# Side taps of a 3x3 convolution: rows read as unbroken runs of 64, column planes swapped by the accumulator's address pattern

## Chip, cores, metric

One core of a Trainium2 chip. The metric is the device time of one execution in microseconds (us); lower is better. A matmul's "spacing" below is the time from its start to the start of the next matmul, taken from the trace's records of starts. PE is TensorE (PEld its weight loads), DVE is VectorE, ACT is ScalarE, POOL is GpSimd.

## The reference, cut to what matters

```python
def reference(x, t_emb, g1, be1, w1, w_emb, g2, be2, w2):   # x: (2, 512, 64, 64) bf16
    ...                                                     # gn: group norm over 4 groups
    def conv3(z, w):                                        # 3x3, padded, 512 -> 512 channels
        zp = jnp.pad(z, ((0, 0), (0, 0), (1, 1), (1, 1)))
        taps = [jnp.einsum("bchw,oc->bohw", zp[:, :, i:i+H, j:j+W], w[:, :, i, j]) ...]
        ...
    h = conv3(_silu(gn(x, g1, be1)), w1)
    h = h + (_silu(t_emb) @ w_emb).reshape(B, C, 1, 1)
    h = conv3(_silu(gn(h, g2, be2)), w2)
    return x + h
```

## The kernel before

The work is cut into 8 chunks (2 convolutions x 2 images x 2 halves) and 4 units of 128 output channels each. Fast-convolution transforms save matmuls: along rows always, along columns from chunk 1 on. In the trace, chunk 0 ends near 90 us, chunks 1 to 3 near 290 us, chunks 4 to 7 at 486 us. DVE makes the transforms, ACT evacuates PSUM and applies silu.

An image row lies in SBUF as 65 fp16 columns: 32 even pixels, one zero, 32 odd pixels. A "plain" group makes 512 outputs (8 rows, even half then odd half) by three matmuls per input block, one for each column tap `kx`. A side tap makes the even outputs from odd pixels and the other way round, so its read takes the second half of each row first:

```python
RW = 65                                     # row pitch, in elements of 2 bytes
def plain_mms(bank, c, k, ct, s):
    ...
    for i, kx in enumerate((0, 2, 1)):      # the two side taps, then the centre
        ...                                 # w: 128x128 weights
        off, st = ((32, -32), (0, 33), (33, -32))[kx]
        rhs = A(vo + off, [[RW, 8], [st, 2], [1, 32]])
        lst.append((Ps(bank, 0, [[1, 512]]), w, rhs, ct == 0 and i == 0, ct == CT - 1 and i == 2))
```

Every operation is recorded with an assumed cost, and a list scheduler fixes the order on each engine before anything is emitted.

## Time and profile before

| | before |
|---|---|
| time, median of 3 runs | 500.62 us (500.51 to 501.32) |
| profiled span | 500.2 us |
| plain matmuls, 512 columns | 1248, of which 832 side taps |
| spacing of first side tap, second side tap, centre (150 to 475 us) | 228, 227.5, 222 ns |
| spacing of 256 columns; of 512 columns in a row (embedding) | 109 ns; 215 ns |

First the page's line of busy time and the row of the granted clock (40 slices of 12.5 us, tenths of full speed), then the groups of PE by form (busy us, mean ns of one, then idle time just before them and who ended it):

```profile
PE 465.6 (93%) x2853; PEld 276.9 (55%) x2853; DVE 434.1 (87%) x856; ACT 382.5 (76%) x614; POOL 37.8 (8%) x66
...
PEclk9999999988599999999999999999999999999996
```

```profile
line engine op names shapes xcount | busy us, mean ns | idle before us <-releasers
L380 PE MATMUL psum<-ar 128*128 128x512 f16 x1248 | 295.5, 390 | 8.7 <-DVE ar L329 4.3 <-DVE fs L442 2.2 <-ACT ar L352 2.1
L380 PE MATMUL psum<-ar 128*128 128x256 f16 x1408 | 164.8, 274 | 0.2 <-ACT ar L352 0.2
```

Busy time by stretch: window, its length, then busy us and instructions of PE, PEld, DVE, ACT and POOL, then granted clock (1.00 is full), busy share of the DMA engines, GB/s:

```profile
136.00:190.00 54.00, 53.75 (x301) 28.93 (x299) 48.38 (x104) 49.92 (x81) 1.08 (x1) 1.00 0.35 113
190.00:245.00 55.00, 55.00 (x309) 29.64 (x309) 50.63 (x107) 45.34 (x86) 4.75 (x9) 1.00 0.60 188
245.00:305.00 60.00, 60.00 (x360) 34.72 (x359) 59.57 (x114) 48.85 (x76) 1.01 (x7) 1.00 0.78 262
...
395.00:450.00 55.00, 55.00 (x399) 38.57 (x397) 52.82 (x84) 40.01 (x48) 6.24 (x8) 1.00 0.69 166
```

PE is full, yet from 245 to 305 us DVE, with 59.57 of 60, is just as full.

```profile
301.64 2.42 DVE L329 TENSOR_TENSOR ar<-ar 128x2048 f16<-128x2048 f16 x3
303.98 0.16 DVE L442 COPY fs<-psum 128x8 f32<-128x8 f32 x1
304.09 0.69 DVE L329 TENSOR_TENSOR ar<-ar 128x1024 f16<-128x1024 f16 x1
```

The copy stands in DVE's stream without a gap, and PE's first matmul into bank 7 starts at 304.19 us, 0.05 us after the copy ends (from the records of starts and ends). PE is just in time for DVE.

### The profile page before, as it was taken

The page shows a single profiled execution, that of the slowest core. Times are in us where ns is not written, and L with a number is a line of the kernel's source. Part 1 is how long each engine was busy: PE and PEld are TensorE (multiplying, and loading weights), DVE is VectorE, ACT ScalarE, POOL GpSimd, SP SyncE. Part 2 cuts the span into 40 slices and gives each one's busy share as a digit, 9 for nine tenths or more (in the row PEclk, how much of TensorE's full clock was granted, in tenths as well). Part 3 has the DMA queues.
Part 4 walks back from the last instruction along what each step waited for, and adds up shares of the span by engine and source line. Part 5 has one row for each costly group of instructions (what it writes and reads, how often), then busy time and mean ns, then how long its engine had stood idle before and what let it go on. Part 6 is the DMA issues. An engine that isn't in the chain of part 4 may idle for free. (4 is left out here: it accounts for less than half of the span.)

```text
span 500.2 us, 8097 instructions
## 1 busy us (share of the span) xinstructions
PE 465.6 (93%) x2853; PEld 276.9 (55%) x2853; DVE 434.1 (87%) x856; ACT 382.5 (76%) x614; POOL 37.8 (8%) x66
## 2 busy tenths in 40 slices
PE   6999999686699999999999999999999999999980
PEld 5744344253345455555554567666666666666660
DVE  1699999997769999997999999997999999985553
ACT  4886899999699978679987887777765888565440
POOL 3100000000100000110000001103011110011000
PEclk9999999988599999999999999999999999999996
DMA  8754463465723336576576887677676768557232
GB/s 330 281 171 113 156 177 111 167 201 164 237 85 120 119 108 180 171 213 237 201 244 219 294 285 206 167 192 135 194 194 187 201 171 247 108 106 150 44 43 43
DMA packets 41064, 87.17 MB, mean 174 GB/s; under 512 B 6464, under 2 KB 16448, under 8 KB 41024
## 3 DMA queue, kind: packets, MB, share of 16 engines
q1 hardware_dynamic: 35808, 77.07, 46.5%
q0 software_dynamic: 4928, 9.59, 12.9%
q8 instruction: 22, 0.36, 0.3%
q14 instruction: 18, 0.15, 0.1%
q10 hardware_dynamic: 288, 0.01, 0.0%
HBM read 62.25 MB, written 31.85 MB: 188 GB/s over the span
## 5 line engine op out<-in xcount | busy, mean ns | idle before, releaser
L380 PE MATMUL psum<-ar 128*128 128x256 f16 (+2 forms) x2737 | 450.4, 326 | 9.0 <-DVE ar L329 4.3
L329 DVE TENSOR_TENSOR ar<-ar 128x1040 f16<-128x1040 f16 (+6 forms) x682 | 404.9, 651 | 39.5 <-ACT ar L352 35.1
L380 PEld LDWEIGHTS <-ar 128*128 128x128 f16 (+1 forms) x2729 | 264.3, 98 | 192.2 <-issue 16.1
L352 ACT ACTIVATE ar<-ar 128x384 bf16<-128x384 bf16 (+6 forms) x206 | 169.6, 854 | 45.6 <-DVE ar L329 41.6
L352 ACT ACTIVATE ar<-psum 128x512 f16<-128x512 f32 (+2 forms) x221 | 153.8, 718 | 51.1 <-PE psum L380 42.3
L352 ACT ACTIVATE ar<-ar,fs 128x2112 f16<-128x2112 bf16 (+1 forms) x32 | 68.6, 2148 | 6.9 <-DMA ar<-h_scr 5.1
L365 POOL DMA_DIRECT2D out_dram<-ar x16 | 19.3, 1207 | 129.1 <-DVE ar L329 129.0
L333 DVE TENSOR_SCALAR ar<-ar 128x512 f16<-128x512 f16 (+2 forms) x72 | 26.0, 382 | 2.0 <-ACT ar L352 2.0
L352 ACT ACTIVATION_READ_ACCUMULATOR ar<-psum 128x1 f32 x96 | 19.6, 204 | 0.0
L451 POOL TENSOR_TENSOR fs<-fs 128x1 f32<-128x1 f32 (+1 forms) x7 | 7.0, 996 | 138.2 <-DVE fs L449 138.2
L380 PE MATMUL psum<-ar,ones_bf 128*128 128x260 bf16 x64 | 9.5, 307 | 4.7 <-DMA ar<-in_x_dram 4.7
L369 POOL MEMSET ar<- 128x65 f16 (+4 forms) x27 | 4.1, 195 | 114.5 <-DVE ar L329 41.9
L380 PE MATMUL psum<-fs,ones_neg 128*128 128x1 f32 (+3 forms) x36 | 5.2, 258 | 7.0 <-DVE fs L982 6.9
L352 ACT ACTIVATION_READ_ACCUMULATOR ar<-ar 128x1 f32 x56 | 11.0, 197 | 0.0
L380 PEld LDWEIGHTS <-ones_bf 128*128 128x128 bf16 x64 | 6.6, 108 | 6.4 <-issue 3.4
L380 PEld LDWEIGHTS psum<-fs,ones_neg 128*128 128x128 f32 x36 | 5.0, 206 | 8.0 <-DVE fs L982 7.2
L365 POOL DMA_DIRECT2D ar<-ar x4 | 3.7, 930 | 72.3 <-DVE ar L329 56.4
L913 DVE SCALAR_TENSOR_TENSOR ar<-psum,ident 128x128 bf16<-128x128 f32 x4 | 1.2, 290 | 5.6 <-PE psum L380 5.6
L993 DVE BATCH_NORM_STATS2 fs<-ar 128x6 f32<-128x512 bf16 x8 | 5.3, 681 | 0.0
L442 DVE COPY fs<-psum 128x2 f32<-128x2 f32 (+1 forms) x7 | 1.1, 161 | 4.5 <-PE psum L380 4.5
L415 DVE CAST fs<-gparm 128x16 f32<-128x16 bf16 x1 | 0.2, 190 | 2.8 <-DMA gparm<-in_params_dram 2.8
L411 ACT ACT_TABLE_LOAD x1 | 1.3, 1283 | 1.7 <-PEq L1135 1.7
(49 smaller groups left out, 23.4 us busy)
## 6 DMA issues: line engine op xcount, KB each, us to landing
ar<-in_w_dram SPq DMA_DIRECT2D x32, 384.0 KB, 3.9
ar<-in_x_dram SPq DMA_DIRECT2D x16, 552.5 KB, 4.0
h_scr<-ar SPq DMA_DIRECT2D x16, 520.0 KB, 3.2
ar<-h_scr SPq DMA_DIRECT2D x16, 520.0 KB, 4.0
out_dram<-in_x_dram SPq DMA_DIRECT2D x32, 260.0 KB, 4.2
out_dram<-ar POOLq DMA_DIRECT2D x16, 520.0 KB, 6.4
u_scr<-ar SPq DMA_DIRECT2D x16, 384.0 KB, 3.2
ar<-u_scr SPq DMA_DIRECT2D x4, 1536.0 KB, 7.6
```

What stands on the lines that cost most here:

```text
L329: pl.op("DVE", 0.075 + 0.000521 * out.n, lambda: nc.vector.tensor_tensor(out=out.ap, in0=a.ap, in1=b.ap, op=op), regs(a, b), regs(out), name)
L333: pl.op("DVE", cost or 0.075 + 0.00026 * out.n, lambda: nc.vector.tensor_scalar(out=out.ap, in0=a.ap, scalar1=s, scalar2=None, op0=ALU.mul ...
L352: lambda: nc.scalar.activation(out=out.ap, in_=a.ap, func=func, scale=sc, **kw), regs(*rr), regs(*ww), name)
L365: lambda: eng.dma_start(out=out, in_=in_, **kw), regs(*r), regs(*w), name, lat=3.2 if sw else None, after=after, sw=sw)
L369: pl.op("POOL" if eng == "gpsimd" else "DVE", 0.08 + 0.0005 * out.n, lambda: e.memset(out.ap, v), (), regs(out), name)
L380: nc.tensor.matmul(out.ap, lhsT=lhsT.ap, rhs=rhs.ap, start=st, stop=sp, skip_group_check=True)
L411: nc.scalar.activation(out=fs[:, WARM:WARM + 1], in_=fs[:, WARM + 1:WARM + 2], func=ACT.Silu)
L415: nc.vector.tensor_copy(out=fs[:, GB:GB + 4 * CT], in_=gparm[:])
L442: pl.op("DVE", 0.16, lambda: V.tensor_copy(out=F(tot, 2 * n).ap, in_=ps.ap), regs(ps), regs(F(tot, 2 * n)), name)
L451: pl.op("POOL", 0.85, lambda: nc.gpsimd.tensor_tensor(out=F(rs, n).ap, in0=N.ap, in1=F(NEGH, n).ap, op=ALU.pow), regs(N), regs(F(rs, n)), ...
L913: pl.op("DVE", 0.3, lambda: nc.vector.scalar_tensor_tensor(out=j2.ap, in0=g.ap, scalar=1.0 / HW, in1=ident[:], op0=ALU.mult, op1=ALU.mult, ...
L993: pl.op("DVE", 0.61, lambda e=e, q=q: nc.vector.bn_stats(out=q.ap, in_=e.ap), regs(e), regs(q), nm)
```

## The change

The side taps read each row as one run of 64 columns. The swap of the halves moves to the write: the accumulator's pattern puts the first 32 columns of a row 32 places up. Values are the same.

```diff
-            off, st = ((32, -32), (0, 33), (33, -32))[kx]
-            rhs = A(vo + off, [[RW, 8], [st, 2], [1, 32]])
-            lst.append((Ps(bank, 0, [[1, 512]]), w, rhs, ct == 0 and i == 0, ct == CT - 1 and i == 2))
+            if kx == 1:
+                rhs, o = A(vo, [[RW, 8], [33, 2], [1, 32]]), Ps(bank, 0, [[1, 512]])
+            else:
+                rhs, o = A(vo + kx // 2, [[RW, 8], [1, 64]]), Ps(bank, 32, [[64, 8], [-32, 2], [1, 32]])
+            lst.append((o, w, rhs, ct == 0 and i == 0, ct == CT - 1 and i == 2))
```

The scheduler's costs depend on sizes alone, so the order on every engine is unchanged, as the two traces confirm (I compared the recorded operations with their dependences and planned starts: all 2736 are equal).

## The prediction

> **What bounds it now.** The profile page: span 500.2 us, PE busy 93%, DVE 87%, ACT 76%. The table of busy time by stretch shows PE at 10.00 of 10 us in nearly every stretch from 130 to 480 us, but DVE at 9.8 to 10.0 in most of them too. Three phases:
> - 20 to 130 us (plain chunk 0): DVE or ACT is full (DVE 9.4 to 10.0 of 10 from 30 to 100 us, ACT 9.3 to 10.0 from 110 to 130); PE is released by DVE or ACT after gaps of 2.1, 3.3, 6.9 and 2.2 us at 96, 102, 127 and 130 us. DVE/ACT bound.
> - 136 to 486 us: PE issues back to back; what its starts lose against the typical spacing adds up to under 1 us. PE bound, with DVE almost level.
> - 486 to 500 us: a tail without matmuls.
>
> **What the change does.** Same instructions in the same order on all engines (the schedule's costs depend on sizes alone). Of 1248 plain matmuls (128x512), the 832 side taps read 8 runs of 64 instead of 16 runs of 32 with a backward step, and write PSUM in blocks of 32 with swapped order instead of 512 in a row. Weights, bytes and results are unchanged.
>
> **Costs, from the starts of consecutive matmuls in the trace** (150 to 475 us):
> - side tap 228 ns and 227.5 ns; centre tap (16 forward runs) 222 ns; an embedding matmul with 512 unbroken columns 215 ns; 256-column matmuls 109 ns. The Trainium skill, "TensorE: Matmul & The Clock Gate", section Back-to-back issue gap, gives N/2.4 + 2.5 ns, so 215.8 and 109.2: the trace agrees. So a forward break costs about 0.45 ns and a backward one about 0.8.
> - Seven forward breaks: 215.5 + 3 = 218.5 ns, if it counts breaks; 221.5 if only skipped columns count. I take 219.5: 8 ns saved per side tap, 832 x 8 = 6.7 us in all.
> - The write side: the skill's "PSUM — Partial Sum Buffer", section Specifications, says any non-contiguous pattern slows matmuls significantly. This trace disagrees: the 256-column matmuls that write blocks of 32 at pitch 64 and those that write 256 in a row are both at 109 ns. I expect the swapped blocks to be free; the backward order is untried here.
>
> **How much is critical.** PE's starts against the ends of what releases them: PE is pinned to DVE (slack about 0.05 us) at 127, 130, 174, 304 and 390 us, after stretches in which DVE has no gap (145 to 174, 245 to 304, 360 to 394). Side taps there only make PE wait longer. Before 130 us nearly nothing counts. Left: about 380 side taps, 380 x 8 = 3.0 us; 0.2 more from early ACT evacuations.
>
> **Predicted: 497.4 us, range 495.2 to 499.9.** Faster by over 2%: 0.02; within 2%: 0.96; slower by over 2%: 0.02.
>
> **What would show it.** Side-tap spacing 218 to 222 ns, centre tap still 222, 256-column 109. PE busy down by about 6 us; PE's waits on DVE near 127, 174, 304 and 390 us each longer by 0.3 to 1.2 us; DVE's busy time unchanged (434 us), its share up. PE's last matmul about 3 us earlier, tail unchanged at 14 us.
>
> **What would make it wrong.** A backward PSUM step that costs as the backward read did (spacing stays 228: no change, or more: slower); spacing near 215 (gain about 5 us); DVE pins that are looser than I read, so more of the 6.7 us comes through; the half clock granted at 122 to 136 us after PE's wait moving or lasting one period (3.4 us) more or less.

## More of the kernel before

The helpers that matter later:

```python
def tt(out, a, b, op, name=""):             # every add of the transforms, on DVE
    pl.op("DVE", 0.075 + 0.000521 * out.n, lambda: nc.vector.tensor_tensor(...), ...)

def gn_chain(layer, b, ct, mes, name, SB=7, slack=2.5, n=1):   # statistics of a group norm
    ...                                     # small matmuls into PSUM bank 7
    pl.op("DVE", 0.16, lambda: V.tensor_copy(out=F(tot, 2 * n).ap, in_=ps.ap), ...)
    ...                                     # a unit's group 5 uses bank 7 too
```

The gaps of DVE from 190 to 245 us look like room. This one, from the timeline of DVE and then of ACT (start, us, what), decided more than I saw when I predicted:

```profile
225.65 3.04 DVE L329 TENSOR_TENSOR ar<-ar 128x512 f16<-128x512 f16 x6
230.65 1.92 DVE L329 TENSOR_TENSOR ar<-ar 128x1040 f16<-128x1040 f16 x3 [1.96 <-ACT ar L352]
```

```profile
225.70 2.37 ACT L352 ACTIVATE ar<-ar 128x384 bf16<-128x384 bf16 x2
227.94 0.22 ACT L352 ACTIVATION_READ_ACCUMULATOR ar<-ar 128x1 f32 x1
228.03 0.62 ACT L352 ACTIVATE ar<-psum 128x512 f16<-128x512 f32 x1
228.51 0.23 ACT L352 ACTIVATION_READ_ACCUMULATOR ar<-psum 128x1 f32 x1
228.60 2.02 ACT L352 ACTIVATE ar<-ar 128x2145 f16<-128x2145 f16 x1
230.48 0.63 ACT L352 ACTIVATE ar<-psum 128x512 f16<-128x512 f32 x1
```

DVE waits 1.96 us for ACT, and ACT has no gap at all in front of the operation that releases it: it has run without one since 218.54 us, when an add of DVE, not PE, released it. ACT is late with its own work. A faster PE should not shorten this wait.

The last view is PE and DVE near 304 us: PE's statistics matmuls (128x8), DVE's copy of them out of bank 7, and the next group of PE that needs that bank.

```profile
303.02 0.51 PE L380 MATMUL psum<-fs,ones_neg 128*128 128x8 f32 x4
303.39 1.42 PE L380 MATMUL psum<-ar 128*128 128x256 f16 x8
```

## The result, and the profile after

The changed kernel took 501.05 us (median of 4 runs, 499.11 to 501.79) against 500.97 us for the kernel before. The ratio is 0.9994, 95% interval 0.9972 to 1.0017. Ratios here are the mean time of one kernel's fast runs over that of the other's of the same rounds, so not quite the ratio of the medians quoted.

| | before | after |
|---|---|---|
| spacing of first side tap, second, centre | 228, 227.5, 222 ns | 222, 223, 222.5 ns |
| 256 columns | 109 ns | 109 ns |
| end of PE's last matmul, profiled run | 486.3 us | 485.9 us |

```profile
PE 463.6 (93%) x2853; PEld 279.9 (56%) x2853; DVE 434.2 (87%) x856; ACT 381.4 (76%) x614; POOL 37.8 (8%) x66
...
PEclk9999999889599999999999999999999999999995
```

```profile
line engine op names shapes xcount | busy us, mean ns | idle before us <-releasers
L380 PE MATMUL psum<-ar 128*128 128x512 f16 x1248 | 293.5, 391 | 10.6 <-DVE ar L329 4.9 <-DVE fs L442 3.5 <-ACT ar L352 2.2
L380 PE MATMUL psum<-ar 128*128 128x256 f16 x1408 | 164.5, 274 | 0.2 <-ACT ar L352 0.2
```

Those two groups tell most of the story: the plain matmuls are busy 2.0 us less (295.5 to 293.5), and idle in front of them grew by 1.9 us (8.7 to 10.6). (Spacing saves more than 2 us; the busy figure also holds the second half-rate period described below.) The 1.3 us more under `DVE fs L442` is the wait near 304 us:

```profile
302.82 0.81 PE L380 MATMUL psum<-ar 128*128 128x256 f16 x6
304.88 1.05 PE L380 MATMUL psum<-ar 128*128 128x512 f16 x4 [1.24 <-DVE fs L442]
```

```profile
302.33 2.42 DVE L329 TENSOR_TENSOR ar<-ar 128x2048 f16<-128x2048 f16 x3
304.67 0.15 DVE L442 COPY fs<-psum 128x8 f32<-128x8 f32 x1
304.79 1.36 DVE L329 TENSOR_TENSOR ar<-ar 128x1024 f16<-128x1024 f16 x2
```

PE now comes early and stands still for 1.24 us. DVE's copy is not earlier but 0.69 us later than before. The gap of DVE near 230 us has not shrunk by a hundredth, and ACT in front of it is as gapless as before:

```profile
226.69 2.70 DVE L329 TENSOR_TENSOR ar<-ar 128x768 f16<-128x768 bf16 x5
231.36 1.92 DVE L329 TENSOR_TENSOR ar<-ar 128x1040 f16<-128x1040 f16 x3 [1.96 <-ACT ar L352]
```

```profile
228.74 0.62 ACT L352 ACTIVATE ar<-psum 128x512 f16<-128x512 f32 x1
229.21 0.23 ACT L352 ACTIVATION_READ_ACCUMULATOR ar<-psum 128x1 f32 x1
229.31 2.02 ACT L352 ACTIVATE ar<-ar 128x2145 f16<-128x2145 f16 x1
231.19 0.62 ACT L352 ACTIVATE ar<-psum 128x512 f16<-128x512 f32 x1
```

```profile
136.00:190.00 54.00, 53.26 (x298) 29.18 (x297) 47.68 (x102) 49.63 (x79) 1.08 (x1) 1.00 0.35 113
190.00:245.00 55.00, 55.00 (x315) 30.55 (x314) 51.28 (x108) 45.06 (x86) 4.75 (x9) 1.00 0.60 188
245.00:305.00 60.00, 58.76 (x357) 34.79 (x356) 58.93 (x114) 48.43 (x77) 1.02 (x7) 1.00 0.77 258
...
395.00:450.00 55.00, 55.00 (x401) 38.99 (x399) 52.74 (x84) 40.02 (x49) 6.25 (x8) 1.00 0.69 167
```

PE lost its full mark from 245 to 305 us (60.00 to 58.76): that is the wait at 304 us.

Since both kernels have the same order, each instruction of one trace can be paired with its twin in the other, and the difference of their starts followed through the run. Negative means earlier than before. The second changed trace is that of `e7_after_again`, the third that of the experiment `d1_short` below:

| near, us (PE / DVE) | after: PE, DVE | e7: PE, DVE | d1: PE, DVE |
|---|---|---|---|
| 87 / 86 | -0.58, -0.51 | -1.10, -1.03 | 0.00, -1.18 |
| 127 / 123 | +0.70, +0.70 | -1.15, -1.14 | -0.23, -0.22 |
| 176 / 174 | +0.69, +0.71 | -2.31, -2.29 | -1.62, -1.55 |
| 250 / 248 | -0.07, +0.70 | -3.07, -2.31 | -6.02, -1.40 |
| 298 / 297 | -0.52, +0.70 | -3.52, -2.31 | -5.00, -1.41 |
| 310 / 310 | +0.65, +0.69 | -2.35, -2.31 | -0.04, -1.42 |
| 347 / 348 | +0.43, +0.69 | -2.57, -2.31 | -1.58, -0.67 |
| 371 / 372 | +0.29, +0.11 | -2.72, -2.89 | -2.61, -1.25 |
| 444 / 434 | -0.19, +0.11 | -3.20, -2.90 | -2.49, -1.26 |
| 481 / 487 | -0.36, -0.35 | -3.36, -3.36 | -3.04, -3.04 |

Three things stand out. DVE's offset is one constant from 136 to 348 us in both changed traces: whatever PE gains there (about 1.2 us from 176 to 298 us), it gives back at 304 us. The saving reaches DVE only after about 357 us, and there both traces gain the same 1.05 us (+0.70 to -0.35; -2.31 to -3.36). And the two traces of one kernel differ by 3 us, nearly all of it made before 140 us; that part is not the taps (0.5 us is there at 20 us already, the rest goes with the clock, below).

### The profile page after: what moved, and what is told of

Same layout as the page of the kernel before. It is cut to its first block, busy times and chain, and to the rows that moved or that the text cites. A ratio compares the mean times of both kernels' runs of the same rounds, so it can differ in the third digit from the quotient of the medians.

```text
span 500.0 us, 8097 instructions
## 1 busy us (share of the span) xinstructions
PE 463.6 (93%) x2853; PEld 279.9 (56%) x2853; DVE 434.2 (87%) x856; ACT 381.4 (76%) x614; POOL 37.8 (8%) x66
## 5 line engine op out<-in xcount | busy, mean ns | idle before, releaser
L380 PE MATMUL psum<-ar 128*128 128x256 f16 (+2 forms) x2737 | 448.1, 326 | 10.8 <-DVE ar L329 4.9
L380 PEld LDWEIGHTS <-ar 128*128 128x128 f16 (+1 forms) x2729 | 267.2, 99 | 188.9 <-issue 20.5
L352 ACT ACTIVATE ar<-ar 128x384 bf16<-128x384 bf16 (+6 forms) x206 | 169.6, 855 | 53.7 <-DVE ar L329 47.8
L352 ACT ACTIVATE ar<-psum 128x512 f16<-128x512 f32 (+2 forms) x221 | 153.4, 718 | 44.9 <-PE psum L380 35.6
L352 ACT ACTIVATE ar<-ar,fs 128x2112 f16<-128x2112 bf16 (+1 forms) x32 | 68.6, 2148 | 5.8 <-DMA ar<-h_scr 3.2
L352 ACT ACTIVATION_READ_ACCUMULATOR ar<-psum 128x1 f32 x96 | 19.7, 205 | 0.0
L352 ACT ACTIVATION_READ_ACCUMULATOR ar<-ar 128x1 f32 x56 | 11.1, 197 | 0.0
L442 DVE COPY fs<-psum 128x2 f32<-128x2 f32 (+1 forms) x7 | 1.1, 159 | 4.4 <-PE psum L380 4.4
```

Of the source, the lines that this page charges most:

```text
L352: lambda: nc.scalar.activation(out=out.ap, in_=a.ap, func=func, scale=sc, **kw), regs(*rr), regs(*ww), name)
L380: nc.tensor.matmul(out.ap, lhsT=lhsT.ap, rhs=rhs.ap, start=st, stop=sp, skip_group_check=True)
```

## The experiments

My theory after this reading: (a) the taps did get shorter, by about 5 ns; (b) DVE and ACT set the pace up to about 350 us, so little comes through; (c) the rest is the clock. The rivals: the saving is not real on PE, or PE itself or the half-rate periods lose it. Kernels that give a wrong result are marked. The calls did not all run on one chip, so ratios are to the kernel before in the same call.

### What a tap's address patterns cost

`e1_read_write` (wrong), from the kernel before; the three taps of a group get three patterns:

```diff
+            row, swap = Ps(bank, 0, [[1, 512]]), Ps(bank, 32, [[64, 8], [-32, 2], [1, 32]])
+            rhs, o = ((A(vo, [[1, 512]]), swap), (A(vo, [[RW, 8], [1, 64]]), row), (A(vo, [[64, 8], [1, 64]]), row))[i]
```

> Wrong result on purpose: the three taps of every plain group get three different patterns, same sizes and order. First: 512 unbroken columns read, swapped blocks of 32 written. Second: 8 runs of 64 at pitch 65 read, 512 in a row written. Third: 8 runs of 64 at pitch 64 (unbroken in memory) read, 512 in a row written. Theory (only breaks in the READ cost, about 0.85 ns each, 7 breaks = 6 to 7 ns; writes are free): start-to-start 215.5, 222, 215.5 ns. Rival (the swapped write costs too, and the 222 of the changed kernel is part write): first 218 to 222, second 217 to 219, third 215.5. Rival (a run boundary of the pattern costs even where memory goes on): third 218 or more.

Measured: 216, 219, 216 ns. A swapped write on an unbroken read is free, and so is a run boundary where memory goes on. But the read of runs of 64 costs 219, not the 222 that it has in the changed kernel. Neither side had all three: the theory expected 222 for the second tap, the rival 218 or more for the first.

`e2_runs` (wrong):

```diff
+            rhs = A(vo, ([[24, 16], [1, 32]], [[25, 16], [1, 32]], [[56, 8], [1, 64]])[i])   # all written in a row
```

> Wrong result on purpose: all writes in a row; reads are first 16 runs of 32 at pitch 24 (starts at multiples of 16 bytes, 15 backward breaks), second 16 runs of 32 at pitch 25 (most starts off that grid), third 8 runs of 64 at pitch 56 (starts on the grid, 7 breaks). Theory (number of breaks in address order counts, alignment does not): 228, 228, 221.5 to 222.5 ns. Rival (what costs is a run that starts inside a 16-byte line): 215 to 217, 228, 215 to 217 ns.

Measured: 216, 222, 216 ns. My theory of breaks fell; the rival had the pattern, but 228 where 222 was measured. Fifteen backward breaks cost nothing when every run starts at a multiple of 16 bytes. At pitch 25, 14 of 16 runs start off that grid (the starts in elements modulo 8 are 0, 1, 2, ...), and 222 - 216 is 6 ns. At pitch 65, 7 of 8 do: 219 - 216 is 3 ns. That is about 0.45 ns a run in both.

`e5_same3a` and `e6_same3b` (wrong) ask why 219 is 222 in the changed kernel: all three taps of a group get one pattern, a different one for each of the four input blocks `ct`.

```diff
+            rhs = A(vo, ([[RW, 8], [1, 64]], [[RW, 8], [1, 64]], [[1, 512]], [[25, 16], [1, 32]])[ct])
+            o = (row, swap, swap, row)[ct]
```

> Wrong result on purpose: now all three taps of a group have one pattern, which differs by input block. Block 0: 8 runs of 64 at pitch 65, written in a row. Block 1: the same read, written swapped. Block 2: 512 unbroken, written swapped. Block 3: 16 runs of 32 at pitch 25, in a row. Spacing of the middle tap. Theory W (a swapped write adds to a read that is off the 16-byte grid): 219, 222, 216, 222 ns. Theory N (a tap costs more when its neighbour's reads are off the grid as well): 222, 222, 216, 228 ns.

Measured (medians of the middle tap): 219, 223, 216, 222 ns. Theory W: the swapped write adds 3 to 4 ns, but only on a read that is off the grid. Theory N fell: neighbours of the same pattern add nothing.

```diff
+            rhs = A(vo + (32, 32, 0, 1)[ct], ([[64, 8], [-32, 2], [1, 32]], [[RW, 8], [-32, 2], [1, 32]],
+                                              [[RW, 8], [33, 2], [1, 32]], [[1, 512]])[ct])   # all written in a row
```

> Wrong result on purpose: as the last run, all written in a row. Block 0: 16 runs of 32 with a backward step, rows at pitch 64, so all starts on the 16-byte grid. Block 1: the side tap of the kernel before (the same backward step, rows at pitch 65). Block 2: its centre tap. Block 3: 512 unbroken from an odd element. Starts off the grid are what costs: 216, 228, 222 (228 under theory N), 216 ns. Backward breaks are what costs: 228, 228, 222, 216 ns.

Measured: 216, 227, 222, 217 ns. The backward read itself is free when rows lie at pitch 64. At pitch 65 it costs 227, which is 5 more than the 222 of other reads with 14 starts off the grid. So both forms of the swap behave alike: free on the grid, and a few ns dearer off it. (The first backward tap after the aligned block took 230 ns, so a neighbour can still shift a tap by 3 ns.) Why the two add up so, no run shows. What follows for the change: reading runs of 64 saves 8 ns, writing swapped gives back 3 to 4 of them, and 5 ns remain.

These four kernels also save PE time (up to 12 ns a side tap). Their single runs took 502.29, 501.16, 498.69 and 499.24 us: again no clear gain from a faster PE. One run each, so no more than a hint; the section on the clock shows a difference between the first two and the last two.

### Where the saving goes: relieve DVE

`e3_before_light` and `e4_after_light` (wrong) cut every in-place add of DVE to half its columns, in the kernel before and in the changed one. The recorded operations and their order stay the same.

```diff
+        h = (lambda r: <r with its last dimension halved>) if <out is a or b> else (lambda r: r.ap)
-        ... nc.vector.tensor_tensor(out=out.ap, in0=a.ap, in1=b.ap, op=op)
+        ... nc.vector.tensor_tensor(out=h(out), in0=h(a), in1=h(b), op=op)
```

> Wrong result on purpose: the kernel before with every in-place VectorE tensor_tensor cut to half its columns, same instructions and order; VectorE's busy time falls by 35 to 50 us. Theory (TensorE and VectorE are co-critical): TensorE alone still holds 136 to 486 us, so only the stretches where it waited for VectorE or ScalarE shrink: 490 to 498 us. Rival (VectorE alone is the bound): 460 us or less.

> Wrong result on purpose: the changed kernel with the same VectorE relief. Theory (the taps did become 4 to 6 ns shorter, and the saving is eaten by VectorE's rigid stream): 3 to 4.5 us less than the relieved kernel before, while the unrelieved pair differs by under 1 us. Rival (the saving is lost elsewhere, in the clock's half-rate periods or in TensorE itself): difference under 1 us here too.

Measured, five runs each: 498.35 us (mean 498.33) and 494.96 us (mean 494.58); the kernel before beside them 500.83. Ratios to it: 0.9952 (0.9939 to 0.9964) and 0.9874 (0.9850 to 0.9897). The first lies just above the 490 to 498 us expected. The change is worth 3.75 us between the means here, within the 3 to 4.5 us expected. The groups of the relieved kernel before, then of the relieved changed one:

```profile
L383 PE MATMUL psum<-ar 128*128 128x512 f16 x1248 | 295.3, 390 | 7.4 <-DVE ar L332 2.9 <-DVE fs L445 2.2 <-ACT ar L355 2.1
```

```profile
L383 PE MATMUL psum<-ar 128*128 128x512 f16 x1248 | 293.1, 391 | 7.4 <-DVE ar L332 2.9 <-DVE fs L445 2.2 <-ACT ar L355 2.1
```

Now the idle time does not grow: 7.4 and 7.4. Paired start by start, PE's offset between these two goes from -0.46 us (139 us) through -1.60 (250) and -2.05 (298) to -3.15 (481), steadily, and DVE's goes with it, from -0.66 to -3.14. So the saving on PE is real, 2.7 us from 139 us on, and it is DVE's load that swallows it otherwise. (The rest of the 3.75 us lies before 139 us, where start and clock differ between runs too.) The first also shows that relieving DVE alone, by 43 us of busy time (434.1 to 390.7), buys only 2.5 us. Neither engine alone is the bound.

### A larger dose on PE

`d1_short` (wrong): the changed kernel with side taps of 7 rows instead of 8.

```diff
-                rhs, o = A(vo + kx // 2, [[RW, 8], [1, 64]]), Ps(bank, 32, [[64, 8], [-32, 2], [1, 32]])
+                rhs, o = A(vo + kx // 2, [[RW, 7], [1, 64]]), Ps(bank, 32, [[64, 7], [-32, 2], [1, 32]])
+                rhs.n = 512     # planned cost and order unchanged
```

> Wrong result on purpose: the changed kernel with 7 instead of 8 rows in every side tap (448 columns, about 27 ns less each on 832 taps, 22 us less TensorE work), same instructions and order. Theory (from about 130 to 347 us VectorE and ScalarE set the pace and swallow what TensorE saves): VectorE's offset against the kernel before stays constant from 140 to 340 us to 1 us or so, and the whole gains 3 to 7 us on the changed kernel. Rival (TensorE is the bound wherever it issues back to back): 14 us or more.

Measured: 498.62 us (mean of four runs 498.84), ratio to before 0.9963 (0.9943 to 0.9984). That is 1.1 us below the changed kernel (499.94 us, the mean of all its 15 runs), less than the 3 to 7 that I expected, for some 23 us less work on PE (a side tap's spacing is 194.5 instead of 222.5 ns). In the pairing PE comes up to 8.65 us early (at 286 us), while DVE stays within 0.2 us of one offset from 137 to 310 us, and at 310 us PE is back at -0.04. Its groups:

```profile
L380 PE MATMUL psum<-ar 128*128 128x448 f16 x832 | 235.5, 365 | 19.6 <-DVE ar L329 12.3 <-DVE fs L442 5.1 <-ACT ar L352 2.1
L380 PE MATMUL psum<-ar 128*128 128x256 f16 x1408 | 165.8, 275 | 6.1 <-ACT ar L352 5.6 <-DVE ar L329 0.4
```

The idle time in front of these two groups is 25.7 us, against 10.8 in the changed kernel. PE was full in the kernel before, and it was not the bound by itself. The dose has a side effect: PE waits 4.07 us (for ACT, up to 292.48 us) and 2.18 us (for DVE, up to 302.77 us), and half-rate periods of 3.413 us follow at 293.3 and 303.6 us, which the changed kernel does not have. They took part of PE's lead, so that DVE keeps its offset is the cleaner evidence here.

### The clock

`e7_after_again` and `g3_after`: the changed kernel unedited, timed again.

> The changed kernel, unedited, timed in more rounds. Theory (TensorE's saving is eaten up to about 357 us and comes through only after it): 0.5 to 1.2 us less than the kernel before, ratio 0.9976 to 0.9990. Rival (nothing comes through): ratio 0.9995 or more.

> The changed kernel unedited, beside them. Its earlier timings differed (ratios 0.9994 and 0.9966). If the half-rate periods of the clock are what differs: runs with a mean clock of 0.975 or more near 498.7 us, of 0.971 near 499.8, of 0.968 near 501.7.

Measured: 498.75 us, ratio 0.9966 (0.9953 to 0.9979), better than expected; and 499.68 us, ratio 0.9981 (0.9963 to 0.9999). The second expectation named three levels by clock before its runs, and its six runs met them to 0.3 us (501.6, 499.5, 498.75 us). With the first call that is 15 runs of the changed kernel, and their mean granted clock sorts them:

| mean granted clock | runs | time, mean (range) |
|---|---|---|
| 0.975 and more | 4 | 498.71 us (498.58 to 498.75) |
| 0.971 to 0.974 | 7 | 499.68 us (499.11 to 500.49) |
| 0.968 | 4 | 501.64 us (501.55 to 501.79) |

The row of the page for `e7_after_again`, to compare with the two shown above:

```profile
PEclk9999999988699999999999999999999999999995
```

In the records of the granted clock, the first changed trace has half-rate periods of 3.413 us at 95.5 and at 102.4 us and one of 13.653 us at 122.9 us. `e7_after_again` has one of 3.413 us at 101.2 us and one of 10.240 us at 121.6 us. All are multiples of 3.413 us, in or just after the stretch where PE waits for DVE and ACT. (A last half-rate stretch, from about 488 us, lies after the last matmul: it costs nothing but counts in the mean.) In the first trace DVE's offset jumps by 1.38 us across the period at 95.5 us (-0.51 to +0.87); in `e7_after_again` PE is back at full rate at 131.9 instead of 136.5 us, and its offset goes from -1.15 us at 127 us to -2.61 at 139.

The Trainium skill ("TensorE: Matmul & The Clock Gate", Part 1) describes half rate after an idle window of about 3413 ns, and windows that run free of the kernel. Records agree with the length of the windows (3.413, 10.24, 13.653 us), but a window need not be all idle. Cut the 16 traces that have clock records into windows of 3.413 us, in step with their half-rate periods: between 12 and 480 us, each of the 50 full-rate windows with half rate after it had PE idle for 1.82 us or more (by the records of its matmuls), and no window that was followed by full rate had over 1.92 us. So the time of a run depends on how the windows fall on PE's waits. The wait of 2.1 to 2.2 us that ends near 95 us lies in one window in the first changed trace (2.17 us idle, then half rate), but is split between two in the kernel before (1.11 and 1.22 us) and in `e7_after_again` (1.58 and 1.25), without half rate after it. That is luck of the phase, and read from traces, not tested.

Half rate can also turn a saving into a loss: `e1_read_write` and `e2_runs` have two half-rate windows from 302 us on, after a longer wait near 304 us (3.68 and 2.90 us); DVE's offset to the kernel before goes from -0.62 to +1.81 us there in the first. `e5_same3a` waits 2.20 us there, split between two windows, and has none.

Runs of the kernel before do not sort that clearly (22 runs at 0.975 and more average 500.65 us, 8 at 0.971 to 0.974 average 501.39, 10 at 0.969 average 500.91). Only a run at 0.974 has a trace, so why the changed kernel pays more for its 0.968 than the kernel before for its 0.969 is not settled.

All 15 runs average 499.94 us, and the 44 runs of the kernel before average 500.87. The gain is about 0.9 us (0.2%), about 1.9 us on runs with a clock of 0.975 and more (498.71 against 500.65), 1.7 at 0.971 to 0.974, and a loss of 0.7 at 0.968 and 0.969.

### Taking single waits away

`c1_gncopy`: the changed kernel, with the copy near 304 us on ACT (correct result).

```diff
-        pl.op("DVE", 0.16, lambda: V.tensor_copy(out=F(tot, 2 * n).ap, in_=ps.ap), ...)
+        if n == 1:
+            pl.op("DVE", 0.16, ...)
+        else:
+            act(F(tot, 2 * n), ps, ACT.Copy, name=name)
```

> Correct result: the changed kernel, with the copy of the statistics out of bank 7 for the second normalisation (and for the second image) on ScalarE instead of VectorE. TensorE's wait of 1.24 us at 304 us should vanish. Theory (VectorE's stream keeps its pace, so TensorE only waits later, at chunk 6's first taps near 390 us): within 0.7 us of the changed kernel. Rival (this wait is what costs the gain): 1.2 us faster than it.

Measured: 497.83 us (mean 497.86), ratio 0.9944 (0.9931 to 0.9956). It beats the kernel before by 2.8 us and the changed one by more than the 0.7 us that I allowed. But the edit is not clean: with one operation moved, the scheduler finds another order on all engines. So its pair was run, with the same recorded schedule but the taps of before, beside a repeat:

> Correct result: the kernel before with the statistics copy on ScalarE, so the schedule of c1_gncopy without the change. If the new schedule alone made c1_gncopy faster: 498 us or less, and the change adds under 0.5 us to it. If the change's saving comes through because the wait near 304 us is gone: 499.5 to 501 us, 2 to 3 us over c1_gncopy.

> c1_gncopy once more, beside its pair and the changed kernel on one chip. 497.3 to 498.5 us; 1 to 1.5 us less than g3_after if the schedule's gain is real.

Measured: `g1_before_gncopy` 500.64 us (mean 500.46, ratio 0.9987, 0.9974 to 1.0000), `g2_after_gncopy` 498.73 us (mean 498.48, ratio 0.9949, 0.9936 to 0.9961). The schedule alone gives 0.6 us or nothing, and the change is worth 1.98 us between the means. `g2_after_gncopy` is 1.6 us below the changed kernel (500.09, the mean of `g3_after`), just over the 1 to 1.5 expected. In the pair of traces PE's lead is -0.81 us at 176 us, passes 304 us without loss, reaches -2.46 at 371, and falls to -1.41 at 407, because PE now waits at 399 us (the groups of `g1_before_gncopy`, then of `g2_after_gncopy`):

```profile
L380 PE MATMUL psum<-ar 128*128 128x512 f16 x1248 | 294.8, 390 | 7.0 <-DVE ar L329 5.3 <-ACT fs L352 1.6
L380 PE MATMUL psum<-ar 128*128 128x256 f16 x1408 | 165.3, 275 | 0.8 <-DVE ar L329 0.8
```

```profile
L380 PE MATMUL psum<-ar 128*128 128x512 f16 x1248 | 291.1, 389 | 7.6 <-DVE ar L329 5.9 <-ACT fs L352 1.6
L380 PE MATMUL psum<-ar 128*128 128x256 f16 x1408 | 165.4, 275 | 1.9 <-DVE ar L329 1.0 <-ACT ar L352 0.9
```

(The 0.9 under `ACT ar L352` in the second line of `g2_after_gncopy` is new; its pair has none.) DVE's offset stays between -0.57 and -0.79 us from 147 to 431 us; both end at -1.70. The expectation for `g1_before_gncopy` would read its time as the saving let through at 304 us. The traces don't say that: from 147 us on DVE gains 0.91 us in this pair, no more than the 1.05 us of the plain pair; what differs lies earlier, where start and clock count. Removing the wait moved it, as the theory of (b) says. `c1_gncopy` is still the best kernel with a correct result here: 498.17 us.

`c4_defer1`: the changed kernel with the second image's statistics and chunk 2's products recorded one unit later, so that PE need not wait near 127 us (correct result).

```diff
-            run_later = list(later)
-            later.clear()
+            run_later = [] if k == 0 and c in (1,) else list(later)
+            if run_later:
+                later.clear()
...
-            if c + 1 < 8:
+            if c + 1 < 8 and not (k == 0 and c in (1,)):
+                if k == 1 and c in (1,):
+                    prod(c + 1, 0)
                 prod(c + 1, k)
```

> Correct result: the changed kernel, but the statistics of the second image and the products of chunk 2 are recorded one unit later, so that TensorE need not wait for them before unit 11's second row group (bank 7). The idle time at 120 to 130 us (7.0 + 2.2 us) and the half-rate period after it should go. Theory (VectorE and ScalarE hold that stretch, TensorE only follows): TensorE's wait moves to chunk 2's first taps at about 170 us and under 2 us are won. Rival (TensorE's wait and its half clock are themselves critical there): 5 us or more.

Measured: five runs of 501.16 to 503.65 us, ratio 1.0033 (1.0018 to 1.0047): slower than before by 0.3%, and slower than the changed kernel; neither theory had that. One more execution took 2713 us and was the profiled one; it is set aside. The edit also gave another order on the engines. So this reordering does not pay, but whether it took PE's wait near 127 us away, and where it lost its 2 to 3 us against the changed kernel, no fast trace shows.

`c7a_pool_w2` and `c7c_pool_f2`: the changed kernel, with part of DVE's adds on POOL (correct results).

```diff
+        pool = name[:3] in ("w2_",)          # c7c: ("f2_",)
+        e = nc.gpsimd if pool else nc.vector
-        pl.op("DVE", ..., lambda: nc.vector.tensor_tensor(...))
+        pl.op("POOL" if pool else "DVE", ..., lambda: e.tensor_tensor(...))
```

> Correct result: the changed kernel with the adds of the second convolution's weight preparation (48 of them, 768 columns, some 26 us of VectorE's time between 100 and 245 us) on GpSimd. Theory: the wait near 174 us goes and VectorE follows TensorE until 245 us; the pins near 304 and 390 us stay, so 0.5 to 1.5 us better than the changed kernel at best. Rival (GpSimd and VectorE get in each other's way when both read SBUF): VectorE's mean time of an add grows and the kernel is slower than before by some us.

> Correct result: the changed kernel with the 24 adds on the fetched second weights (1024 columns, some 16 us of VectorE's time between 245 and 304 us) on GpSimd. Theory: the wait near 304 us goes and VectorE keeps up with TensorE through chunk 3: 1 to 2.5 us better than the changed kernel. Rival (GpSimd and VectorE get in each other's way): slower.

Measured: 538.25 us and 541.14 us, 7.5% and 8.0% slower. The rival holds. In `c7a_pool_w2`, an add of 512 columns on DVE takes 709 ns on average (426 in the changed kernel), and the moved add of 768 columns takes POOL 1749 ns where DVE took 550; the line of DVE in the changed kernel, then those of DVE and POOL here:

```profile
L329 DVE TENSOR_TENSOR ar<-ar 128x512 f16<-128x512 f16 x72 | 28.1, 426 | 0.2 <-ACT ar L352 0.2
```

```profile
L332 DVE TENSOR_TENSOR ar<-ar 128x512 f16<-128x512 f16 x72 | 48.3, 709 | 0.4
```

```profile
L332 POOL TENSOR_TENSOR ar<-ar 128x768 f16<-128x768 f16 (+1 forms) x48 | 83.2, 1749 | 126.5 <-ACT ar L354 86.7 <-DMA ar<-in_x_dram 16.2 <-issue 15.2
```

The Trainium skill ("SBUF — State Buffer", Who interferes with whom) says that a DVE instruction with two SBUF inputs contends with a GpSimd instruction that reads SBUF; the longer adds agree. How much of the 37 to 40 us is that, how much the slower adds themselves, and how much the other order that the scheduler chose was not separated.

## Why the prediction was wrong

The time that was forecast, 497.4 us (495.2 to 499.9), was not met: 501.05 in the call that counts, 499.94 over all runs of the changed kernel.

- **"8 ns saved per side tap, 832 x 8 = 6.7 us in all": mis-sized.** The mean of the side taps went from 227.75 to 222.5 ns, so about 5 ns, and the centre tap lost about half a nanosecond: near 4 us in all. The step that failed is "a forward break costs about 0.45 ns and a backward one about 0.8". Breaks do not cost; runs that start off the 16-byte grid do (`e2_runs`, `e6_same3b`). I read a price per break from two patterns that differ in alignment, order and count at once. That the read alone came out at 219 ns, near my 219.5, is luck: seven breaks happened to go with seven starts off the grid.
- **"I expect the swapped blocks to be free": half wrong.** Free on an unbroken read (216 ns, `e1_read_write`), 3 to 4 ns on this one (`e5_same3a`). The evidence that I gave, 256-column matmuls with unbroken reads, could not show that.
- **"Left: about 380 side taps, 380 x 8 = 3.0 us": the step that failed, beside the size.** At 5.25 ns these taps would give 2.0 us. I found where PE is pinned to DVE (at 174 and 304 us rightly, the waits there grew to 0.74 and 1.24 us; near 390 us none grew), but counted the taps between 174 and 245 us as gained, since DVE has gaps there. I took those gaps for waits on PE through ACT. They are waits on ACT, which is behind with its own work, so DVE does not move when PE does: its offset is constant from 136 to 348 us. What comes through is about 0.5 to 0.6 us before 96 us, against my "nearly nothing", and 1.05 us after 357 us. `d1_short` shows the same with a dose five times as large, and the relieved pair shows the saving whole again.
- **The half-rate periods** were named as a risk of one period, 3.4 us, more or less. In the runs with the lowest clock they took what was left: 501.64 against 498.71 us by the clock of the run. With a gain of 1 to 2 us and such a spread, a range of 4.7 us that left out 500 was too sure.
- **Right**: DVE's busy time unchanged (434.1 and 434.2 us), 256-column matmuls at 109 ns, the class "within 2%". **Wrong**: "PE's last matmul about 3 us earlier" (0.36 us in the first trace; 3.36 in `e7_after_again`, about half of that from the clock and a 0.5 us earlier start), the wait near 127 us did not grow (6.92 and 6.96 us), and PE's busy time fell by 2.0 us (5.4 in `e7_after_again`) instead of 6.

## What to carry to other kernels

A full engine is not yet the bound: before a gap of its neighbour is counted as room, follow it to the engine that ended it, and look whether that one was idle, waiting for yours, or late with its own work. To know what a saving is worth, make it five times as large with a wrong result, and relieve the rival engine in both versions: two cheap runs that went far to settle it here. Look at the clock records of such runs, since a longer wait can bring half rate. Time per matmul followed where its runs start here, so measure read and write patterns together, in the combination that will be used.

## What the Trainium skill lacked or had wrong

- "PSUM — Partial Sum Buffer", Specifications: that any non-contiguous pattern slows matmuls significantly did not hold here. Swapped blocks of 32 on an unbroken read: 216 ns, as for 512 in a row. With a read off the grid they add 3 to 4 ns of 219, under 2%.
- "SBUF — State Buffer", Door 1 (the note on cachelines): that crossing into a new 16-byte line costs agrees with the runs, and they give the size for a matmul's moving operand: about 0.45 ns for each run that starts off the grid (219 ns for 7 such runs, 222 for 14, 216 for none). One unbroken run from an odd element costs 217. Backward steps on the grid are free (216).
- No page has the joint cost: a backward read (227 ns against 222) or a swapped write (223 against 219) is dearer only when the runs are off the grid.
- "TensorE: Matmul & The Clock Gate", Back-to-back issue gap: N/2.4 + 2.5 ns (109.2 and 215.8) agrees with 109 and 215 to 216 ns. That page's sustained figure of about 131 ns for N = 512 does not: matmuls with a weight load each keep 215 to 228 ns here.
- The same page, Part 1, has the half-rate periods and their windows of 3413 ns right, but half rate did not need a whole idle window: the 50 windows that brought it had PE idle for 1.82 to 3.41 us, and a wait of 2.17 us was enough where it fell into one window. It gives figures from run to run for the ramp at the start of a kernel. Here periods in mid-kernel go with a spread of 3.2 us in 500 between runs of one kernel (498.58 to 501.79), more than the gain that was to be measured.
- The same page warns of a clock stuck at a quarter for 50 us and more. One execution of `c4_defer1` took 2713 us with 512-column matmuls at a mean of 1698 ns instead of about 390, while DVE kept its pace (adds of 1024 columns at 694 ns, 691 in the changed kernel). Its trace holds no clock record, so the 1.00 that the views print is no measurement, and whether this was that state is open. The page names a counter to check against, which no run here has; the spacing shows the state at once (mostly 1279 ns instead of 222).
